# Linear attention and an MLP mixer: a new order of batch 1's first steps, new gates on the later quarters of w_ch2, token mixing of batch 1 in two parts

## The chip, the core and the metric

The kernel runs on one core of one Trainium2 chip. The core has five engines with an instruction queue each: PE (TensorE, matmuls; its weight loads are listed as PEld), DVE (VectorE), ACT (ScalarE), POOL (GpSimd) and SP (SyncE, here only an issuer of transfers). Transfers run on the core's 16 DMA engines, whoever issues them. The metric is the device time of one execution in microseconds, the median of several runs.

## The reference

For each of 8 batches, linear attention over 8 heads (576 rows, 64 columns a head), and then a mixer block: token mixing across the 576 rows, channel mixing across the 512 columns.

```python
def phi(x): return np.where(x > 0, x, np.exp(x) - 1.0) + 1.0
q_p, k_p = phi(q), phi(k)
kv  = einsum('bhsd,bhse->bhde', k_p, v)
z   = sum(k_p, axis=2)
num = einsum('bhsd,bhde->bhse', q_p, kv)
den = einsum('bhsd,bhd->bhs', q_p, z)[..., None] + 1e-06
x   = (num / den) as [batch, 576, 512]
h   = relu(x.T @ w_tok1) @ w_tok2        # w_tok1 576 x 256, w_tok2 256 x 576
u   = x + h.T
out = u + relu(u @ w_ch1) @ w_ch2        # w_ch1 512 x 1536, w_ch2 1536 x 512
```

All inputs and the output are float32 in memory; matmuls run in bfloat16 and sum in float32.

## The kernel before

**Tiles.** A batch's 576 rows are four tiles of 128 rows and a fifth, half full, of 64 (r = R = 4). The eight heads are two halves c = 0, 1 (loads, phi, transposes, kv), and a load of half of q, k or v is 576 KB. w_ch1 and w_ch2 are loaded in four quarters of 384 KB (as bfloat16); a quarter of w_ch2 holds three of the twelve row blocks kc, so quarter 1 is kc 0 to 2, quarter 2 is kc 3 to 5, quarter 3 is kc 6 to 8 and quarter 4 is kc 9 to 11.

**The steps of a batch.** phi (lines 146 to 170) takes exp on ACT (L149), an add and max on DVE (L155) and a min on DVE (L163). vcast (L174) casts v to bfloat16. qtr (lines 210 to 215) transposes phi(q) on PE (L200) and copies it from PSUM (L207). kv (lines 182 to 196) multiplies phi(k) by v, 72 small matmuls (L189), and copies the result on ACT (L195). nd (lines 223 to 246) does numerator and denominator of some row tiles of one half: matmuls (L230), then on DVE an add, a reciprocal and a product (L239, L241, L242) that writes x. mm1 (lines 297 to 306) is the first half of token mixing, ten matmuls (L303) over the five row tiles and a relu on ACT (L306); mm2_half (lines 343 to 361) is the second. mm3 (L531) and mm4 (L571) are channel mixing, whose results are evicted by ACT (L538) or DVE (L535) and, at the end, by mm4_end (L599).

**The order.** The program is written out by hand and each engine works through its own list in order. In the stage of the change, batch 0's channel mixing is the main work (the list `big`, lines 1007 to 1009: indices 0 to 11 are mm3 of the blocks mc, 12 to 23 are mm4 in the order of kc) and batch 1's first steps are put after numbered members of it (`at0` and `fill`, lines 1010 to 1028). The first two members of mm4, 12 and 13, do kc 0 and 1 for two row tiles each; 14 to 23 do one kc for all four row tiles, four matmuls each. They sum in four PSUM banks, the same four that mm3's blocks used. For batch 1 the order on PE before the change is: kc 0 and 1 (12 and 13), first transposes of q, kc 2, second transposes, kv, kc 3, nd00, kc 4, nd01, kc 5, nd10, kc 6, nd11, kc 7, nd20, kc 8, nd21, kc 9, mm1, kc 10, kc 11, mm2_half. The nd names give the pair of row tiles (0, 1, or 2 for the last tile) and the half.

**The transfers.** SP issues the loads of q, k and v in the order k, q, v for batch 1 (lines 956 to 958), then q, k, v for batch 2 (lines 960 to 962). POOL issues the weights' loads, since those are cast on the way. `after` (line 119) adds a wait for another transfer's landing. Before the change, batch 1's k waits for the first quarter of w_ch1, quarter 2 of w_ch2 waits for the first half of batch 1's q, quarters 3 and 4 follow it in POOL's list without a wait of their own, and the first half of batch 2's q waits for quarter 2.

## Time and profile before

| | |
|---|---|
| median of 3 runs | 250.88 us (250.22 to 251.24) |
| the profiled execution | 250.88 us, of which the traced span is 249.1 us |
| PE busy | 238.4 us (96% of the span), 2396 matmuls |
| DVE, ACT, POOL busy | 185.8, 140.7, 66.1 us |
| granted PE clock | 1.00 of full speed |
| read from memory, written | 35.85 MB, 9.44 MB |
| w_ch loads (8 of 384 KB), from issue to landing, median | 10.0 us |
| loads of k, q and v (halves), from issue to landing, medians | 6.0, 5.9 and 9.7 us |

The profile is of one execution. A line of the timeline gives the start in the span, the time from the first start to the last end of the merged instructions, the engine, the line of the kernel, the operation with what it writes and reads, and in brackets how long the engine had been idle and which work released it. Matmuls overlap: one of 128 x 512 is listed with 0.38 us, but four in a row start 0.86 us after each other. A line of the chain that ended last has the start, the duration, and the engine or transfer. A line of the windows has the stretch, its length, the busy time and the number of instructions of PE, PEld, DVE, ACT and POOL, the granted clock, the DMA share and the GB/s.

### The profile page before, as it was taken

The page shows a single profiled execution, that of the slowest core. Times are in us where ns is not written, and L with a number is a line of the kernel's source. Part 1 is how long each engine was busy: PE and PEld are TensorE (multiplying, and loading weights), DVE is VectorE, ACT ScalarE, POOL GpSimd, SP SyncE. Part 2 cuts the span into 40 slices and gives each one's busy share as a digit, 9 for nine tenths or more (in the row PEclk, how much of TensorE's full clock was granted, in tenths as well). Part 3 has the DMA queues.
Part 4 walks back from the last instruction along what each step waited for, and adds up shares of the span by engine and source line. Part 5 has one row for each costly group of instructions (what it writes and reads, how often), then busy time and mean ns, then how long its engine had stood idle before and what let it go on. Part 6 is the DMA issues. An engine that isn't in the chain of part 4 may idle for free.

```text
span 249.1 us, 5884 instructions
## 1 busy us (share of the span) xinstructions
PE 238.4 (96%) x2396; PEld 154.7 (62%) x2418; DVE 185.8 (75%) x328; ACT 140.7 (56%) x225; POOL 66.1 (27%) x76
## 2 busy tenths in 40 slices
PE   7799989999899999999999999999999999999994
PEld 3485445564768545765588545765577556888673
DVE  5984676889998378967594398858893859877853
ACT  4765681569775268745997168655953561275100
POOL 9750030296901700061004500051006100430000
PEclk9999999999999999999999999999999999999999
DMA  6999999999738994699938956699052702452036
GB/s 236 262 203 258 340 259 294 372 249 288 302 23 211 264 368 146 91 267 360 320 93 189 397 152 219 130 323 260 21 129 37 170 1 45 63 120 52 0 87 168
DMA packets 49771, 48.39 MB, mean 194 GB/s; under 512 B 30032, under 2 KB 35536, under 8 KB 49744
## 3 DMA queue, kind: packets, MB, share of 16 engines
q1 hardware_dynamic: 41648, 35.00, 48.6%
q0 software_dynamic: 7472, 12.22, 22.4%
q10 hardware_dynamic: 624, 0.79, 1.0%
q8 instruction: 19, 0.31, 0.5%
q14 instruction: 8, 0.07, 0.1%
HBM read 35.85 MB, written 9.44 MB: 182 GB/s over the span
## 4 chain that ended last, share of the span: by engine, by line
PE 76%; DMA 11%; DVE 5%; POOL 3%; issue 3%; SPq 0%; POOLq 0%; DVEq 0%
PE ps L780 22%; PE ps L531 21%; DMA wc<-in_moe_w_ch_dram 6%; PE ps L303 6%; DMA q_raw<-in_q_dram 5%; PE ps L571 5%; PE ps L316 4%; PE ps L734 4%; PE ps L704 4%; PE ps L558 2%; PE ps L580 2%; PE ps L545 2%; DVE y L155 2%; PE ps L259 1%; PE ps L189 1%
## 5 line engine op out<-in xcount | busy, mean ns | idle before, releaser
L531 PE MATMUL ps<-uT,wc 128*128 128x512 bf16 x332 | 76.0, 379 | 0.5 <-issue 0.2
L538 ACT ACTIVATE cr<-ps 128x512 bf16<-128x512 f32 x79 | 45.9, 600 | 32.9 <-PE ps L531 32.5
L531 PEld LDWEIGHTS <-wc 128*128 128x128 bf16 x336 | 32.0, 98 | 37.9 <-issue 1.1
L791 POOL TENSOR_TENSOR obuf<-obuf,q_raw 128x512 f32<-128x512 f32 x6 | 7.6, 1269 | 94.7 <-ACT w L785 74.5
L789 DVE TENSOR_TENSOR obuf<-ps,u 128x512 f32<-128x512 f32 x24 | 16.3, 687 | 11.8 <-PE ps L780 8.8
L780 PE MATMUL ps<-k_raw,v_raw 128*128 128x256 bf16 x216 | 24.9, 273 | 0.0
L780 PEld LDWEIGHTS <-cr 128*128 128x128 bf16 x216 | 21.1, 98 | 4.5
L780 PEld LDWEIGHTS <-v_raw 128*128 128x128 bf16 x216 | 21.0, 98 | 3.9 <-issue 0.4
L149 ACT ACTIVATE e<-q_raw 128x1152 bf16<-128x1152 f32 x16 | 18.2, 1159 | 8.1 <-DMA q_raw<-in_q_dram 8.1
L149 ACT ACTIVATE e<-k_raw 128x1152 bf16<-128x1152 f32 x16 | 18.2, 1163 | 3.9 <-DMA k_raw<-in_k_dram 3.8
L654 DVE TENSOR_TENSOR v_raw<-cr 128x768 bf16<-128x768 bf16 (+2 forms) x24 | 14.9, 619 | 5.0 <-ACT cr L538 5.0
L272 DVE TENSOR_TENSOR x<-ps,dens 128x768 bf16<-128x768 f32 x18 | 17.2, 958 | 0.6
L780 PE MATMUL ps<-wc,cr 128*128 128x256 bf16 x144 | 17.7, 273 | 0.0
L328 DVE TENSOR_TENSOR u<-ps,x 128x1024 bf16<-128x1024 f32 x12 | 14.7, 1222 | 1.8 <-PE ps L316 1.5
L155 DVE TENSOR_SCALAR y<-k_raw 128x1152 bf16<-128x1152 f32 x16 | 11.9, 769 | 4.8 <-DMA k_raw<-in_k_dram 4.8
L163 DVE TENSOR_TENSOR qp<-e,y 128x1152 bf16<-128x1152 bf16 x16 | 11.9, 756 | 3.6 <-ACT e L149 2.8
L163 DVE TENSOR_TENSOR kp<-e,y 128x1152 bf16<-128x1152 bf16 x16 | 11.8, 753 | 3.5 <-ACT e L149 3.4
L155 DVE TENSOR_SCALAR y<-q_raw 128x1152 bf16<-128x1152 f32 x16 | 13.4, 850 | 1.0 <-DMA q_raw<-in_q_dram 0.9
L303 PE MATMUL ps<-x,w 128*128 128x512 bf16 x49 | 13.8, 379 | 0.3
L174 ACT CAST vs<-v_raw 128x1152 bf16<-128x1152 f32 x12 | 13.5, 1160 | 0.0
L571 PE MATMUL ps<-wc,cr 128*128 128x512 bf16 x47 | 12.0, 379 | 1.0 <-DVE cr L535 0.7
L316 PE MATMUL ps<-ar,w2p 128*128 128x512 bf16 x44 | 11.6, 379 | 0.3
(161 smaller groups left out, 386.2 us busy)
## 6 DMA issues: line engine op xcount, KB each, us to landing
k_raw<-in_k_dram SPq DMA_DIRECT2D x16, 576.0 KB, 6.0
q_raw<-in_q_dram SPq DMA_DIRECT2D x16, 576.0 KB, 5.9
v_raw<-in_v_dram SPq DMA_DIRECT2D x14, 576.0 KB, 9.7
out_dram<-obuf POOLq DMA_DIRECT2D x12, 512.0 KB, 6.8
wc<-in_moe_w_ch_dram POOLq DMA_DIRECT2D x8, 384.0 KB, 10.0
out_dram<-obuf POOLq DMA_DIRECT2D x4, 256.0 KB, 5.2
cr<-in_v_dram POOLq DMA_DIRECT2D x2, 288.0 KB, 7.9
out_dram<-obuf POOLq DMA_DIRECT2D x4, 128.0 KB, 7.6
```

Of the source, the lines that this page charges most:

```text
L149: nc.scalar.activation(out=e, in_=f, func=AF.Exp)
L155: nc.vector.tensor_scalar(out=y, in0=f, scalar1=1.0, scalar2=1.0, op0=ALU.add, op1=ALU.max)
L163: live["phi"] = nc.vector.tensor_tensor(out=dst.transpose([0, 2, 1, 3]), in0=e.rearrange("p (i t d) -> p i t d", i=nj, t=T), in1=y.rearran ...
L272: nc.vector.tensor_tensor(out=xv[:, :, rc0:rc0 + 3], in0=v_[:, :, k0:k0 + 6, 0:D].rearrange("p i (q a) d -> p i q a d", a=2), in1=den[:, : ...
L303: nc.tensor.matmul(out=ps[:, mt], lhsT=w1t[:, b, ms] if r == R else w1[:, r, ms], rhs=x[b][:, r, :], start=(r == 0), stop=(r == R))
L316: nc.tensor.matmul(out=ps[:, i], lhsT=w2v(kt, r, b), rhs=ar[b][:, kt, :], start=(kt == 0), stop=(kt == NT - 1 and not add))
L531: nc.tensor.matmul(out=ps, lhsT=wc1[:, kj, 128 * mc:128 * mc + 128], rhs=uTj[b][:, kj] if n < 2 else uT[b][:, :, kj], start=(kj == 0), sto ...
L538: nc.scalar.activation(out=cr[b][:, mc, :], in_=ps, func=AF.Relu)
L571: nc.tensor.matmul(out=ps, lhsT=crt[:, kc, :] if t == 8 else cr[b][:, kc, 128 * r:128 * r + 128], rhs=wc2[:, kc, :], start=(kc == 0), stop ...
L654: nc.vector.tensor_tensor(out=s_[which - 1][:, ks], in0=x_, in1=y_, op=op)
L780: nc.tensor.matmul(out=live[tile_][:, j], lhsT=lhs[:, k_], rhs=rhs[:, k_], start=(first and j == 0 and k_ == 0), stop=(k_ == KH - 1), skip ...
L789: nc.vector.tensor_tensor(out=o, in0=live[tile_], in1=u[n % 2][:, d::2, HC[c]], op=ALU.add)
```

## The change

It has four parts.

1. Batch 1's steps take other places among the members of `big`. The order on PE becomes: kc 0 and 1, first transposes of q, kc 2, kc 3, second transposes, kc 4, kv, kc 5, nd00, kc 6, nd01, kc 7, nd10, nd11, kc 8, nd2, kc 9, mm1 without the last row tile, mm1's last row tile, kc 10, kc 11, mm2_half.
2. The last row tile's numerator and denominator are done for both halves at once (`nd_last`), and mm1 is issued in two parts: all row tiles but the last for both column blocks (8 matmuls), and then the last row tile (2 matmuls) and the relus.
3. The copies of the second transposes are split between DVE and ACT (they were both on DVE), and the cast of v's second half is split, one pair of heads on DVE and one on ACT (it was all on ACT).
4. Quarter 2 of w_ch2 waits for the second half of batch 1's k, quarter 3 for the first half of its v (POOL's list keeps their order, and quarter 4 follows), and the first half of batch 2's q waits for the second half of batch 1's v.

```diff
--- before.py
+++ after.py
@@ -169,8 +169,8 @@
         phi_add(nm, n, 2 * c, 2)
         phi_end(nm, n, 2 * c, 2)
 
-    def vcast(n, c, copy=nc.scalar.copy):
-        js = slice(2 * c, 2 * c + 2)
+    def vcast(n, c, copy=nc.scalar.copy, js=None):
+        js = slice(2 * c, 2 * c + 2) if js is None else slice(js[0], js[-1] + 1)
         copy(out=vs[:, js, :, 0:D],
              in_=raw["v", rb(n)][:, js].rearrange("p j (t d) -> p j t d", t=T))
 
@@ -207,12 +207,12 @@
         put(out=v_[:, :, c, ts[0]:ts[-1] + 1].transpose([0, 2, 1, 3]),
             in_=tp[:, 0:len(ts)].rearrange("p t (a s) -> p t a s", a=2))
 
-    def qtr(n, c, put=nc.scalar.copy):
+    def qtr(n, c, put=2 * [nc.scalar.copy]):
         tp = two16()
         for h, ts in enumerate(TS):
             qtr_mm(c, ts, tp[:, h])
         for h, ts in enumerate(TS):
-            qtr_put(n, c, ts, tp[:, h], put)
+            qtr_put(n, c, ts, tp[:, h], put[h])
 
     def qtr_dma(n):
         for a in range(2):
@@ -244,6 +244,24 @@
                 "p r (h d) -> p r h d", h=HG),
             in0=v_[:, :, :, 0:D],
             in1=den[:, :, :, None].to_broadcast([128, m, HG, D]), op=ALU.mult)
+
+
+    def nd_last(n):
+        b = n % 2
+        ps = banks()
+        for c in range(2):
+            o = ps[:, c, 0:4 * D1].rearrange("p (i a e) -> p a i e", i=2, a=2)
+            for a in range(2):
+                t0 = D * (T * (2 * a + c) + 2 * R - b)
+                nc.tensor.matmul(out=o[:, a], lhsT=qT[b][:, t0:t0 + 128], rhs=kvbd[b][:, c, a],
+                                 start=True, stop=True)
+        v_ = ps[:, :, 0:HG * D1].rearrange("p c (h e) -> p c h e", h=HG)
+        den = work.tile([128, 2, HG], FP32, name="den", tag="den")
+        nc.vector.tensor_scalar(out=den, in0=v_[:, :, :, D], scalar1=EPS, scalar2=None, op0=ALU.add)
+        nc.vector.reciprocal(out=den, in_=den)
+        nc.vector.tensor_tensor(
+            out=x[b][:, R].rearrange("p (c h d) -> p c h d", c=2, h=HG), in0=v_[:, :, :, 0:D],
+            in1=den[:, :, :, None].to_broadcast([128, 2, HG, D]), op=ALU.mult)
 
 
 
@@ -294,15 +312,17 @@
         at = D * (T * kt + 2 * r - (b if r == R else 0))
         return w2p[:, at:at + 128]
 
-    def mm1(n):
+    def mm1(n, rs=range(R1)):
         b = n % 2
-        ps = banks(4 if n > 1 else None)
+        if rs[0] == 0:
+            live["mm1"] = banks(4 if n > 1 else None)
+        ps = live["mm1"]
         for mt in range(NT):
             ms = slice(128 * mt, 128 * mt + 128)
-            for r in range(R1):
+            for r in rs:
                 nc.tensor.matmul(out=ps[:, mt], lhsT=w1t[:, b, ms] if r == R else w1[:, r, ms],
                                  rhs=x[b][:, r, :], start=(r == 0), stop=(r == R))
-        for mt in range(NT):
+        for mt in range(NT) if rs[-1] == R else ():
             nc.scalar.activation(out=ar[b][:, mt, :], in_=ps[:, mt], func=AF.Relu)
 
     def mm2(n, rs, add=False):
@@ -956,24 +976,26 @@
     for nm in "kqv":
         for c in range(2):
             landed[nm + "1", c] = load(nm, 1, c, c_in[0] if nm == "k" and c == 0 else None)
-    c2_in += [after(load_wc2(i), landed["q1", 0] if i == 1 else None) for i in range(1, NB)]
+    c2_in += [after(load_wc2(i), landed[{1: ("k1", 1), 2: ("v1", 0)}[i]] if i < 3 else None) for i in range(1, NB)]
     for nm in "qkv":
         for c in range(2):
-            load(nm, 2, c, c2_in[1] if nm == "q" and c == 0 else None)
+            load(nm, 2, c, landed["v1", 1] if nm == "q" and c == 0 else None)
 
 
     def steps(n):
 
         out_ = [("kv", lambda: kv(n, range(2)))] if n < 2 else []
         if n == 1:
-            puts = [nc.scalar.copy, nc.vector.tensor_copy if n == 1 else nc.scalar.copy]
+            puts = [2 * [nc.scalar.copy], [nc.vector.tensor_copy, nc.scalar.copy]]
             out_ += [(f"qt{c}", lambda c=c: qtr(n, c, puts[c])) for c in range(2)]
-        for i, rs in enumerate(([0, 1], [2, 3], [4])) if n < 2 else ():
+        for i, rs in enumerate(([0, 1], [2, 3])) if n < 2 else ():
             for g in range(2):
                 out_.append((f"nd{i}{g}", lambda g=g, rs=rs: nd(n, g, rs)))
+        if n < 2:
+            out_ += [("nd2", lambda: nd_last(n)), ("mm1a", lambda: mm1(n, range(R)))]
         if n > 1:
             out_.append(("nd", lambda: nd_all(n)))
-        out_.append(("mm1", lambda: mm1(n)))
+        out_.append(("mm1", lambda: mm1(n, range(R1) if n > 1 else [R])))
         if n > 1:
             out_ += [("mm2a", lambda: mm2(n, [0, 1])), ("mm2b", lambda: mm2(n, [2, 3]))]
             if n % 2:
@@ -1007,20 +1029,22 @@
     big = [lambda mc=mc: mm3(0, mc, range(2, 4), dve=mc == 3) for mc in range(4)] + \
         [lambda mc=mc: mm3(0, mc, dve=mc in (6, 9)) for mc in range(4, NCH)] + \
         [lambda kc=kc: m4_0(kc) for kc in range(NCH)]
-    at0 = {"qt0": 13, "qt1": 14, "vc": 13, "kv": 14, "nd00": 15, "nd01": 16, "nd10": 17,
-           "nd11": 18, "nd20": 19, "nd21": 20, "mm1": 21}
+    at0 = {"qt0": 13, "vc0": 15, "qt1": 15, "vc1": 15, "kv": 16, "nd00": 17, "nd01": 18,
+           "nd10": 19, "nd11": 19, "nd2": 20, "mm1a": 21, "mm1": 21}
     fill = []
     for ex, ad, en, nm, c in ((2, 2, 3, "k", 0), (5, 5, 6, "k", 1), (8, 8, 9, "q", 0),
                               (11, 11, 12, "q", 1)):
         fill += [(ex, lambda nm=nm, c=c: phi_exp(nm, 1, 2 * c, 2)),
                  (ad, lambda nm=nm, c=c: phi_add(nm, 1, 2 * c, 2)),
                  (en, lambda nm=nm, c=c: phi_end(nm, 1, 2 * c, 2))]
-    late = [("vc", lambda: vcast(1, 0, nc.vector.tensor_copy)), ("vc", lambda: vcast(1, 1))]
+    late = [("vc0", lambda: vcast(1, 0, nc.vector.tensor_copy)),
+            ("vc1", lambda: vcast(1, 1, nc.vector.tensor_copy, [2])),
+            ("vc1", lambda: vcast(1, 1, nc.scalar.copy, [3]))]
     fill += [(21, lambda g=g: phi("q", 2, g)) for g in range(2)]
     fill += [(22, lambda: qtr_dma(2)), (22, lambda: load_all(3, "q"))]
     fill += [(22, lambda: weight_sums((tf, B12, B11), (tb[1], B22, tf)))]
     first = steps(1)
-    for nm, fn in first[1:2] + late + first[2:3] + first[0:1] + first[3:]:
+    for nm, fn in first[1:2] + late[:1] + first[2:3] + late[1:] + first[0:1] + first[3:]:
         fill += [(at0[nm], fn)]
     fill += [(23, fn) for fn in (
         lambda: mm4_end(0, 0), lambda: mm4_end(0, 1), lambda: mm2_half(1, 0),
```

## The prediction

> **What bounds the kernel now.** I read the page's busy row first, then the chain that ended last in order of time, then the PE timeline around the changed steps, then who waited there. The first row says where to look:
>
> ```profile
> PE 238.4 (96%) x2396; PEld 154.7 (62%) x2418; DVE 185.8 (75%) x328; ACT 140.7 (56%) x225; POOL 66.1 (27%) x76
> ```
>
> TensorE is the bound, and its granted clock is 1.00 in every stretch from 20 to 42 us, so only its idle time or its work can change the end. From 54 us on the chain is nearly all PE, so a shift X of batch 1's end shifts the end of the kernel by X. The chain shows two transfers ahead of the place that is changed:
>
> ```profile
> 18.97 12.43 DMA q_raw<-in_q_dram
> ...
> 31.93 5.87 DMA wc<-in_moe_w_ch_dram
> 37.80 0.04 issue
> 37.84 0.38 PE ps L571
> ```
>
> The reader sees q of batch 1 (first half) land at 31.40, the second quarter of w_ch2 issued at 31.93 because of that landing, and PE's block kc=3 released by it at 37.84. The PE timeline gives every gap:
>
> ```profile
> 31.79 0.39 PE L571 MATMUL ps<-wc,cr 128*128 128x512 bf16 x1
> 32.83 1.67 PE L571 MATMUL ps<-wc,cr 128*128 128x512 bf16 x7 [0.65 <-DVE cr L535]
> 34.34 0.67 PE L200 MATMUL ps<-identity,qp 128*128 128x128 bf16 x9
> 34.84 1.03 PE L571 MATMUL ps<-wc,cr 128*128 128x512 bf16 x4
> 35.71 0.67 PE L200 MATMUL ps<-identity,qp 128*128 128x128 bf16 x9
> 36.30 0.48 PE L189 MATMUL ps<-vs,kp 64*64 64x65 bf16 x36
> 37.11 0.48 PE L189 MATMUL ps<-vs,kp 64*64 64x65 bf16 x36 [0.32 <-ACT vs L174]
> 37.84 1.02 PE L571 MATMUL ps<-wc,cr 128*128 128x512 bf16 x3 [0.25 <-DMA wc<-in_moe_w_ch_dram]
> 38.70 0.40 PE L230 MATMUL ps<-kvbd,qT 128*128 128x130 bf16 x4
> ```
>
> Matmuls overlap, so I take a cost from start to start. In the chain four L571 take 0.86 us, so a block of mm4 is 0.86. Nine transposes are 0.50 (34.34 to 34.84), 72 kv matmuls 0.71, four nd matmuls 0.24, ten mm1 matmuls 2.15. The stretch from the first L571 (31.79) to the first matmul of mm2_half (48.95) is 17.16 us. Its work is 12 x 0.86 + 2 x 0.50 + 0.71 + 5 x 0.24 + 2.15 = 15.38. So PE idles 1.78 us there: 0.82 at 31.79 to 32.83 (less one matmul of 0.22), 0.45 before 37.11 (36.30 + 0.36), 0.37 before 37.84, and crumbs. **That is all the change can win.**
>
> **Part 1: the order on PE.** Nothing is removed but one of six nd rounds in name: nd2 issues the same four matmuls as nd20 and nd21, so PE's work stays 15.38. On DVE it replaces 2 x (0.16 + 0.18 + 0.42) by 0.17 + 0.20 + 0.69, 0.46 less, beside PE blocks: the nd chain on DVE ends at 45.23 and mm1 reads the last row tile only at 45.92. The split of the second q transpose's copies (DVE 0.41, ACT 0.69 or 0.59 in the L207 rows) and of v's cast (half of DVE's 0.758, half of ACT's 1.16) is worth nothing while kv is late for another reason; without that it cuts 0.5 us from the wait before 37.11. The 0.82 stays: the DVE eviction L535 stands behind phi's add, which waited for q's landing at 31.40, and both come before anything moved. The moves are: block kc=3 ahead of the second transposes, kc=4 ahead of kv. So kc=3 is wanted at 32.83 + 1.51 + 0.50 + 0.86 = 35.70 instead of 37.47, and kc=6, behind nd00 and no longer behind nd10, one block and one nd earlier relative to kv. Kv now has two blocks (1.72 us) of cover for its v.
>
> **Part 2: the queues.** Here the sum is decided. The trace's landing records (16 completions of each transfer, one by each DMA engine) show one engine about 1 us behind the others: k of batch 1, second half, 27.08 to 27.51 on fifteen, 28.43 on the last; v, second half, to 34.92 and 35.87. Landing means that last engine. It ends q at 31.40 and 33.02, v at 34.44 and 35.87, and the second to fourth quarters at 37.80, 39.69, 41.82: a half of q or v costs it 1.42 us alone, a quarter 1.9, and it never rests. So an earlier request there does not add bandwidth; it only changes the order.
>
> New gates: quarter 2 after k's second half (28.43) instead of q's first half (31.40), hence issued at 28.43 + 0.53 (the 31.40 to 31.93 of before) = 28.96. When does that engine take it up? Issued at 31.93 it landed at 37.80, so its 1.9 us began at 35.9, 3.9 after the issue, with v's transfers running. The lower end: at once behind the first quarter, which ends at 31.74. I take 28.96 + 3.9 = 32.9, the row that is the same transfer under the same load. From there it shares with v. Sharing has rows too: between 28.43 and 31.40 a half took 2.97 instead of 1.42, beside the first quarter, which took 4.2 for itself (27.54, the end of the small transfer ahead of it, to 31.74). So quarter 2 lands at 32.9 + 4.2 = 37.1, v's first half at 33.02 + 2.97 = 36.0 instead of 34.44, and v's second at 33.02 + 1.42 + 1.43 + 1.9 = 37.8, some 38.0 with the loss of sharing. Quarter 3 is new in its gate: after v's first half, 36.0 + 0.53 = 36.5, where it had been issued at 32.69. Its landing: at best when that engine is free, 38.0 + 1.9 = 39.9; at worst 5.87 after the issue, 42.4 (or 42.9 where v is at 36.5). Between them stands the row of the other fifteen engines: they landed quarter 2 at 36.47 to 36.89, 4.8 after its issue although idle by 34.9. I take 36.5 + 4.8 = 41.3. While the queue starts up, the DMA share falls:
>
> ```profile
> 30.00:32.00 2.00, 1.91 (x8) 0.70 (x8) 1.07 (x2) 1.18 (x3) 0.07 (x1) 1.00 1.05 402
> 32.00:34.00 2.00, 1.35 (x7) 0.57 (x6) 2.00 (x4) 2.00 (x4) 2.00 (x3) 1.00 0.94 325
> 34.00:36.00 2.00, 2.00 (x22) 1.29 (x21) 1.41 (x3) 1.85 (x4) 0.36 (x1) 1.00 0.92 170
> ```
>
> The last number is GB/s: 402 falls to 170 as POOL's three quarters (issued 31.93 to 34.35) begin. The new gates let POOL start this twice. Behind quarter 3's wait on POOL stand only quarter 4 (wanted by kc=9, four blocks later) and work from 48.4 on. q of batch 2 now waits for v's second half (38.0) instead of quarter 2 (37.80): no change for SP's queue, whose later loads follow it, and none for exp on ACT, which had it at 43.95.
>
> The Trainium skill, "DMA: Bandwidth & Descriptors", section "Anatomy of one DMA — SWDGE (gpsimd) path", gives about 2.0 us plus bytes by 436 GB/s for such a transfer, by which 384 KB take an estimated 2.9 us against the 5.87 of the chain; by it quarters 2 and 3 would land near 32 and 38, nothing but the 0.82 would be left of the stalls, and the time would be near 250.0. The row is under load and I go by the row. The same page, section "Queues, rings and completion order", has each DMA engine go round robin between queues by packet, which speaks against this change, since quarter 2 then holds up v; the 2.97 against 1.42 agrees.
>
> **The sum.** Block kc=2 ends at 35.70 and kc=3 waits to 37.1 (1.4, new). Then kc=3 37.96, transposes 38.46, kc=4 39.32, kv without a wait (v's casts done by 38.0 + 0.65 = 38.7) 40.03, kc=5 40.89, nd00 41.15 (its kvbd copies, 0.76 on ACT, are hidden by kc=5). kc=6 waits for quarter 3 until 41.3 (0.15). From there to mm2_half: six blocks 5.16, four nd 0.96, mm1 2.15 = 8.27, with DVE's nd rounds (1.07 each) done at 45.8, under mm1a. So mm2_half begins at 49.6 instead of 48.95: +0.65, some +0.7 with crumbs. The profiled execution is 250.88 (span 249.1 and 1.78 around it), which is also the median shown. **Forecast 251.6 us**, +0.3%. The waits of 0.45 and 0.37 are removed and one of 1.4 put in their place.
>
> **Rivals.**
> - A, the gain: quarter 2 begins at 31.74 and lands at 31.74 + 4.2 = 35.9, so kc=3 waits 0.2. v's halves land at 36.5 and 38.0, kv waits some 0.2 for the last cast (38.7), kc=6 is reached at 40.2, and quarter 3 is there (39.9). mm2_half at 40.2 + 8.27 = 48.5: -0.45, 250.4; with no stall but the 0.82, -0.95, 249.9. For it: the ring is free for it by order of issue. Against: the 3.9 us from issue to work of the same transfer.
> - B, slower: quarter 3 decides. It is wanted at 40.2 to 41.2, earlier than the 41.30 of before, and asked for at 36.5 to 37.0 instead of 32.69. If it needs the 5.87 of quarter 2, it lands at 42.4 to 42.9 and mm2_half is at 50.7 to 51.2: +1.7 to +2.2, 252.6 to 253.1, centre 252.8. It costs anything from a landing at 40.7 (48.95 - 8.27) and over 0.5% from 41.95. For it: the dip in the windows, and q of batch 2 arriving at 40 beside it. Against: v is over by 38, so that nothing need hold it.
> - C, the change does not do what it says: quarter 2 still lands at 37.8 behind v. Then the order alone acts: kc=3 from 37.84, kc=6 at 41.85, mm2_half at 50.1: +1.2, 252.1. Against: it is issued 3 us earlier.
>
> **How the numbers follow.** Forecast 0.42, A 0.20, B 0.30, C 0.08. Half a per cent (1.25 us) is about what a measurement of this kernel can tell from no change. Slower by more: B nearly whole (0.28), half of C and the tail of the forecast (0.05), 0.33. Faster by more asks for a gain of 1.25 out of 1.78 with the 0.82 kept, so it is left 0.05. Within: 0.62. The range takes in A's centre and B's upper half: 250.2 to 253.0.
>
> **What would show it.** In the new PE timeline: the gaps before 37.11 and 37.84 gone; a gap of about 1.4 before kc=3 released by the DMA of wc (step right; 0.2 is A, 2.1 is C); the gap at 32.83 still 0.82 (larger: quarter 2 came early enough to hold up q, which I priced at nothing); a gap before kc=6, after nd00, released by wc (0 to 0.5 forecast, over 1 is B). The first POOL issue at 28.96, the second where v's first half lands, 36.0. I am wrong if quarter 2 is taken up within 2 us of its issue, or if the stages after 54 us do not simply shift.

## The result and the profile after

The changed kernel takes **254.22 us** (median of 4 runs, 253.15 to 254.41), beside 251.06 us (250.22 to 251.30) of the kernel before: ratio 1.0123, 95% interval 1.0086 to 1.0161. It is 3.2 us slower; 251.6 was forecast, and the measured time lies above the range of 250.2 to 253.0. Here and below medians and ranges are of all executions, but ratios and intervals only of those within 1.5% of the fastest of the same kernel, which leaves out the profiled executions of e2, e6 and e12, so that of these only the stretch up to 66 us is read. The profiled execution of the changed kernel is 253.15 us (span 251.4), 2.27 us above that of before. In it the lines have moved by up to 20: mm3 is L551, mm4 L591, mm2_half L372, POOL's sums L661.

The row of the busy times shows the same work, 1.0 us more of it listed on PE in a span 2.3 us longer:

```profile
PE 239.4 (95%) x2396; PEld 155.0 (62%) x2418; DVE 185.9 (74%) x325; ACT 140.8 (56%) x226; POOL 66.4 (26%) x76
```

The chain that ended last passes through quarter 2 of w_ch2, as before, and now also through a transposing transfer of u in batch 2:

```profile
18.43 10.33 DMA k_raw<-in_k_dram
29.30 7.86 DMA wc<-in_moe_w_ch_dram
37.20 1.02 PE ps L591 x4
...
83.32 3.62 DMA uT<-u
86.98 1.90 PE ps L551 x8
```

Quarter 2 is asked for at 29.30 instead of 31.93 and lands at 37.16 instead of 37.80. A request 2.63 us earlier brought 0.64 us. The PE timeline of the changed kernel in the stage of the change:

```profile
31.92 1.95 PE L591 MATMUL ps<-wc,cr 128*128 128x512 bf16 x8
33.70 0.67 PE L200 MATMUL ps<-identity,qp 128*128 128x128 bf16 x9
34.20 1.03 PE L591 MATMUL ps<-wc,cr 128*128 128x512 bf16 x4
37.20 1.02 PE L591 MATMUL ps<-wc,cr 128*128 128x512 bf16 x4 [1.97 <-DMA wc<-in_moe_w_ch_dram]
38.06 0.67 PE L200 MATMUL ps<-identity,qp 128*128 128x128 bf16 x9
38.56 1.03 PE L591 MATMUL ps<-wc,cr 128*128 128x512 bf16 x4
39.52 0.99 PE L189 MATMUL ps<-vs,kp 64*64 64x65 bf16 x72
...
44.16 0.40 PE L230 MATMUL ps<-kvbd,qT 128*128 128x130 bf16 x4 [0.19 <-DVE x L242]
...
50.23 0.27 PE L372 MATMUL ps<-x,identity 128*128 128x256 bf16 x1
```

The gap of 0.82 at kc 0 and 1 is gone, and so are the two ahead of kv's second half and of kc=3. In their place stands one gap ahead of kc=3: block kc=2 ends at 35.06 (34.20 + 0.86) and kc=3 starts at 37.20, **2.1 us** later (the bracket counts 1.97, from the modelled end of the last matmul). kv is listed in one piece with 0.99, and there is no gap ahead of kc=6 at 41.60. mm2_half begins at 50.23 instead of 48.95, **+1.28**. At 68.27, where the last 32 small matmuls on the row tails (the fifth tiles) of batches 0 and 1 start behind batch 2's numerators and denominators, it is +1.97, and from 87 us to the end a constant +2.24.

The windows show the same dip in what is moved while POOL's transfers start, 142 GB/s where it was 170, with the DMA share at 1.06 or more:

```profile
32.00:34.00 2.00, 2.00 (x15) 0.99 (x14) 1.50 (x3) 2.00 (x4) 0.10 (x1) 1.00 1.12 319
34.00:36.00 2.00, 1.23 (x11) 0.60 (x9) 1.43 (x2) 1.24 (x3) 1.77 (x2) 1.00 1.07 142
36.00:38.00 2.00, 0.80 (x4) 0.38 (x4) 0.00 (x0) 0.00 (x0) 0.00 (x0) 1.00 1.06 174
```

In the last of the three, PE has four matmuls in 2 us, and DVE, ACT and POOL do nothing while it waits for the transfer.

### The profile page after: what moved, and what is told of

It is laid out like the page before. It is cut to its first block, busy times and chain, and to the rows that moved or that the text cites. A ratio compares the mean times of both kernels' runs of the same rounds, so it can differ in the third digit from the quotient of the medians.

```text
span 251.4 us, 5884 instructions
## 1 busy us (share of the span) xinstructions
PE 239.4 (95%) x2396; PEld 155.0 (62%) x2418; DVE 185.9 (74%) x325; ACT 140.8 (56%) x226; POOL 66.4 (26%) x76
## 4 chain that ended last, share of the span: by engine, by line
PE 75%; DMA 12%; DVE 5%; POOL 3%; issue 2%; ACT 1%; SPq 0%; POOLq 0%; DVEq 0%
PE ps L551 22%; PE ps L800 21%; DMA wc<-in_moe_w_ch_dram 7%; PE ps L323 6%; DMA k_raw<-in_k_dram 4%; PE ps L336 4%; PE ps L754 4%; PE ps L724 4%; PE ps L591 3%; PE ps L578 2%; PE ps L600 2%; PE ps L565 2%; PE ps L189 2%; PE ps L277 2%; DMA uT<-u 1%
## 5 line engine op out<-in xcount | busy, mean ns | idle before, releaser
L551 PE MATMUL ps<-uT,wc 128*128 128x512 bf16 x332 | 76.0, 379 | 1.2 <-DVE cr L555 0.6
L551 PEld LDWEIGHTS <-wc 128*128 128x128 bf16 x336 | 32.0, 98 | 38.9 <-issue 1.9
L155 DVE TENSOR_SCALAR y<-k_raw 128x1152 bf16<-128x1152 f32 x16 | 12.5, 806 | 5.4 <-DMA k_raw<-in_k_dram 5.4
L591 PE MATMUL ps<-wc,cr 128*128 128x512 bf16 x46 | 11.6, 379 | 2.2 <-DMA wc<-in_moe_w_ch_dram 2.0
L174 ACT CAST vs<-v_raw 128x1152 bf16<-128x1152 f32 (+1 forms) x12 | 13.0, 1120 | 0.0
```

The source lines that it names most:

```text
L155: nc.vector.tensor_scalar(out=y, in0=f, scalar1=1.0, scalar2=1.0, op0=ALU.add, op1=ALU.max)
L551: nc.tensor.matmul(out=ps, lhsT=wc1[:, kj, 128 * mc:128 * mc + 128], rhs=uTj[b][:, kj] if n < 2 else uT[b][:, :, kj], start=(kj == 0), sto ...
L591: nc.tensor.matmul(out=ps, lhsT=crt[:, kc, :] if t == 8 else cr[b][:, kc, 128 * r:128 * r + 128], rhs=wc2[:, kc, :], start=(kc == 0), stop ...
```

## The theories

**T1, the order.** kc=3 now stands ahead of the second transposes and of kv, so PE comes to it 2.4 us sooner in the program (35.06), and quarter 2 lands near 37 whatever its gate. The wait is the loss, and what hangs on batch 1's steps makes it grow.

**T2, the gates (rival).** The new gates slow the transfers of q and v, or let quarter 2 and v hold each other up; with the old gates the new order would cost nothing.

**T3, the later stage (rival).** The loss at the end arises mainly after 55 us, between DVE and POOL or at the transposing transfer of u, and the stage of the change only sets it off.

A table for what follows, each row from one profiled execution, in us from the start of its span: landing of the first half of batch 1's q, landing of quarter 2, PE's longest gap between kc=2 and kc=5, start of mm2_half, and start of the last 32 small matmuls on the row tails (L545 or L565). The last column is the ratio of the times to those of the kernel before on the same chip.

| kernel | q | quarter 2 | gap | mm2_half | row tails | ratio [95%] |
|---|---|---|---|---|---|---|
| before | 31.40 | 37.80 | 0.32 | 48.95 | 66.30 | |
| changed | 30.29 | 37.16 | 1.97 | 50.23 | 68.27 | 1.0123 [1.0086, 1.0161] |
| e0 | 30.11 | 36.77 | 1.95 | 49.85 | 67.87 | 1.0136 [1.0087, 1.0185] |
| e1 | 31.07 | 37.29 | 1.79 | 50.37 | 68.40 | 1.0132 [1.0080, 1.0184] |
| e2 | 30.93 | 37.34 | 1.88 | 49.78 | 67.13 | 1.0040 [1.0003, 1.0078] |
| e3 | 30.04 | 36.43 | 1.50 | 49.51 | 66.97 | 1.0088 [1.0055, 1.0122] |
| e4 | 30.34 | 36.56 | 0.32 | 47.70 | 65.57 | 1.0024 [0.9993, 1.0055] |
| e5 | 31.03 | 37.25 | 0.60 | 48.90 | 66.22 | 1.0009 [0.9974, 1.0044] |
| e6 | 30.32 | 36.73 | none | 47.67 | 65.70 | 1.0029 [0.9999, 1.0059] |
| e8 | 31.57 | 35.67 | none | 50.67 | 68.01 | 1.0145 [1.0097, 1.0192] |
| e9 | 30.06 | 36.78 | 0.32 | 47.93 | 65.28 | 0.9987 [0.9971, 1.0004] |
| e11 | 30.63 | 36.84 | 0.60 | 48.62 | 65.93 | 0.9997 [0.9968, 1.0026] |
| e12 | 30.08 | 36.62 | none | 47.71 | 65.73 | 1.0048 [1.0010, 1.0087] |
| e13 | 30.53 | 37.09 | none | 48.21 | 65.68 | 1.0012 [0.9980, 1.0045] |
| e14 | 30.51 | 37.44 | none | 48.61 | 66.08 | 0.9994 [0.9967, 1.0022] |
| e15 | 30.39 | 36.96 | none | 47.83 | 65.86 | 0.9989 [0.9966, 1.0012] |

e10 left no profile that can be read; its ratio is 1.0095 [1.0069, 1.0121].

## The experiments

**e0: the changed kernel again.**

> The changed kernel once more, for a second profile and more times, since its profiled execution (253.15 us) lay 1 us below its other three (254.1 to 254.4). Theory (PE waits for the second quarter of w_ch2): 253 to 254.5 us; the new profile again has a gap of 1.5 to 3 us on PE ahead of block kc=3, released by the transfer of wc, and the quarter lands at 37 to 38 us. Rival (the queues themselves, two separate starts of POOL's transfers): the gap stands ahead of kc=6 or in the loads of batch 2 in this one.

Measured: 254.12 us (252.55 to 255.11). The gap ahead of kc=3 is 1.95, quarter 2 landed at 36.77. The loss and its place are those of the first profile.

**e1: the new order alone.** Order, `nd_last` and splits as changed, gates as before.

```diff
-    c2_in += [after(load_wc2(i), landed[{1: ("k1", 1), 2: ("v1", 0)}[i]] if i < 3 else None) for i in range(1, NB)]
+    c2_in += [after(load_wc2(i), landed["q1", 0] if i == 1 else None) for i in range(1, NB)]
-            load(nm, 2, c, landed["v1", 1] if nm == "q" and c == 0 else None)
+            load(nm, 2, c, c2_in[1] if nm == "q" and c == 0 else None)
```

> The new order, nd_last, mm1 in two parts and the split copies, with the old gates of the transfers. Theory: quarter 2 lands at 37.8 as before the change, kc=3 is wanted at some 35.5 and waits 2.3 us, everything behind it on PE is later by 0.6 us than in the changed kernel: 253.5 to 255 us. Rival (the gates cost the time): the gates are the old ones, so the time is that of the kernel before, 250.5 to 251.5.

Measured: 254.23 us, the whole loss. Its PE timeline has the same gap at the same place, although quarter 2 was asked for 2.3 us later (31.61):

```profile
34.52 1.03 PE L591 MATMUL ps<-wc,cr 128*128 128x512 bf16 x4
37.34 1.02 PE L591 MATMUL ps<-wc,cr 128*128 128x512 bf16 x4 [1.79 <-DMA wc<-in_moe_w_ch_dram]
```

The gates neither cause the loss nor soften it. T2 falls.

**e2: the new gates alone.** The kernel before with the two gate lines of the change (e1's diff, the other way round).

> The old order with the new gates. Theory: kv's second half waits for v until about 37.5 (0.5 us more than before), kc=3 follows at 37.9 and finds its quarter landed at 37.2: 250.5 to 251.5 us. Rival (the gates cost the time): 252.5 us and more, with a wait for quarter 3 ahead of kc=6.

Measured: 252.80 us, ratio 1.0040. v's second half lands at 36.97 instead of 35.87, held up by quarter 2, and ACT's undivided cast of it holds up kv; kc=3 comes behind it and finds its quarter there:

```profile
35.83 0.48 PE L189 MATMUL ps<-vs,kp 64*64 64x65 bf16 x36
38.20 0.48 PE L189 MATMUL ps<-vs,kp 64*64 64x65 bf16 x36 [1.88 <-ACT vs L174]
38.61 1.04 PE L571 MATMUL ps<-wc,cr 128*128 128x512 bf16 x4
```

The gates alone move the wait from one transfer to the other. The time is above the forecast of 250.5 to 251.5, but the rival's wait ahead of kc=6 is not there, and by the ratios the gates cost less than the order.

**e5: the old places.** Gates as before (e1's lines), every step back at its old place among the blocks; `nd_last`, mm1 in two parts and the splits stay.

```diff
-    at0 = {"qt0": 13, "vc0": 15, "qt1": 15, "vc1": 15, "kv": 16, "nd00": 17, "nd01": 18,
-           "nd10": 19, "nd11": 19, "nd2": 20, "mm1a": 21, "mm1": 21}
+    at0 = {"qt0": 13, "vc0": 13, "qt1": 14, "vc1": 14, "kv": 14, "nd00": 15, "nd01": 16,
+           "nd10": 17, "nd11": 18, "nd2": 19, "mm1a": 21, "mm1": 21}
```

> The old gates and the old places of the transposes, v's casts, kv and the nd rounds; new are only nd_last, mm1 in two parts and the split copies and casts. Theory (the places of kc=3 and kc=4 ahead of the second transposes and kv are what costs): the time of the kernel before, 250.5 to 251.5, kv's second half 0.3 us sooner, kc=3 at 37.8 as before. Rival (the last row tile in one round and mm1 in two parts, or the split, cost): 252.5 us and more, with gaps on PE around mm1.

Measured: 250.53 us beside 249.91 (ratio 1.0009, [0.9974, 1.0044]): the kernel before. With e1 this puts the loss in the places, and prices `nd_last`, mm1's two parts and the splits at nothing that can be measured.

**e6: the new order without the wait.** In the changed kernel, blocks kc 3 to 5 of batch 0 read the first quarter's rows instead of quarter 2's, which are there; the product of three row blocks of w_ch2 is left out, one taken twice.

```diff
-                rhs=wc2[:, kc, :], start=(kc == 0), stop=(kc == NCH - 1))
+                rhs=wc2[:, kc - 3 if wait and 3 <= kc < 6 else kc, :],
+                start=(kc == 0), stop=(kc == NCH - 1))
```

> The changed kernel, but blocks kc=3 to 5 of batch 0 multiply the first quarter of w_ch2 instead of the second, so nothing on PE waits for quarter 2 there (the part left out: the product of three row blocks of w_ch2 with batch 0). All transfers and all instructions are those of the changed kernel. Theory (PE's wait for quarter 2 is the loss): no gap ahead of kc=3; kv then waits for v's second half (36 us and its casts), some 0.3 us; mm2_half 1.5 to 2 us sooner than in the changed kernel and the end 2 to 2.5 us sooner, 251 to 252 us. Rival (the transfers' new order costs in itself, elsewhere): 253.5 us and more.

Measured: 250.84 us, ratio 1.0029 [0.9999, 1.0059]. kc=2 and kc=3 are one row of 8 matmuls, and mm2_half starts at 47.67, 2.56 earlier than in the changed kernel:

```profile
33.77 1.89 PE L591 MATMUL ps<-wc,cr 128*128 128x512 bf16 x8
35.49 0.67 PE L200 MATMUL ps<-identity,qp 128*128 128x128 bf16 x9
...
47.67 0.27 PE L372 MATMUL ps<-x,identity 128*128 128x256 bf16 x1
```

So the wait for quarter 2 is most of the loss, and T1 holds for it. Everything else in the change, the late v included, comes to 0.3%, with an interval from nothing to 0.6%. What follows mm2_half does not go away with the wait: from mm2_half to the row tails it is 18.03 here and 18.04 in the changed kernel, against 17.35 in the kernel before.

**e8: quarter 2 without a gate.** The changed kernel, quarter 2 asked for at 16.67 behind the first quarter.

```diff
-    c2_in += [after(load_wc2(i), landed[{1: ("k1", 1), 2: ("v1", 0)}[i]] if i < 3 else None) for i in range(1, NB)]
+    c2_in += [after(load_wc2(i), landed["v1", 0] if i == 2 else None) for i in range(1, NB)]
```

> The changed kernel without any gate on quarter 2 of w_ch2: POOL issues it right behind quarter 1, ahead of batch 1's loads. Theory (the slowest DMA engine is busy without a pause until 38 us, so an earlier quarter 2 makes q and v later by the 1.9 us that it takes): quarter 2 lands at 33 to 34 us and there is no gap ahead of kc=3, but q's first half lands at 32 to 33 and PE waits before kc=0 (0.82 before, 0 to 0.5 in the changed kernel) for 1 to 2 us, and kv waits for v at 37.5 to 38: 252.5 to 254.5 us, no better than the changed kernel by more than 1 us. Rival (the late quarter 2 is a mere question of its gate): 250 to 251.5 us, no gaps.

Measured: 254.28 us, no better than the changed kernel. Quarter 2 lands at 35.67, 1.5 earlier (33 to 34 was expected), and the price is paid by all others: q 31.57 and 33.72, v 35.83 and 37.13, quarter 3 40.77 (39.05 in the changed kernel), quarter 4 45.88 (41.69). Its PE timeline has three smaller gaps for the one that went:

```profile
33.01 1.67 PE L591 MATMUL ps<-wc,cr 128*128 128x512 bf16 x7 [0.79 <-DVE cr L555]
...
40.81 1.02 PE L591 MATMUL ps<-wc,cr 128*128 128x512 bf16 x4 [0.36 <-DMA wc<-in_moe_w_ch_dram]
...
45.92 0.38 PE L591 MATMUL ps<-wc,cr 128*128 128x512 bf16 x1 [1.07 <-DMA wc<-in_moe_w_ch_dram]
```

So the request that was moved forward moved the others back, and the time is the same.

**e3: POOL's first sums earlier.** POOL's "sums" are differences of blocks of w_ch2. In the changed kernel, the first six, which wait for phi(q) of batch 2, wait for its first half instead of its second.

```diff
-    fill += [(21, lambda g=g: phi("q", 2, g)) for g in range(2)]
+    def phi_q2(g):
+        phi("q", 2, g)
+        if g == 1:
+            live["phi"] = live["phi_q2"]
+        live["phi_q2"] = live["phi"]
+
+    fill += [(21, lambda g=g: phi_q2(g)) for g in range(2)]
```

> The changed kernel, but POOL's first six differences of w_ch2 blocks wait for the first half of phi(q) of batch 2 instead of the second, so POOL begins them some 1.5 us earlier. Theory (the DVE op on k of batch 2 at 56.13 us took 1.59 instead of 0.98 us because POOL's last difference was still running): that op is 0.8 to 1.0 us long again and the end comes 0.6 us sooner than in the changed kernel, unless POOL then lengthens the DVE ops on q of batch 2 by as much. Rival (it is later for PE's sake, POOL is beside it): no change, within 0.2 us in the profile.

Measured: 253.59 us, ratio 1.0088, beside 1.0136 of e0 (the intervals overlap, so at the end the gain is not shown). The first add of phi(k) of batch 2 takes 0.89 us instead of 1.59, and the 0.69 that the changed kernel loses between mm2_half and the row tails (50.23 to 68.27 against 48.95 to 66.30 is 18.04 against 17.35) is gone: 49.51 to 66.97 is 17.46. But the collision came back at another place. The last minimum of phi(q) of batch 2 now runs beside POOL's first sums and takes twice its 0.76:

```profile
48.79 1.52 DVE L163 TENSOR_TENSOR qp<-e,y 128x1152 bf16<-128x1152 bf16 x1
...
55.53 1.56 DVE L155 TENSOR_SCALAR y<-k_raw 128x1152 bf16<-128x1152 f32 x2
```

**e4: POOL's sums later.** The kernel before, with a POOL memset of 0.52 us ahead of its first sums.

```diff
+        if abc[0][0] is tf and not live.get("pad"):
+            live["pad"] = after(nc.gpsimd.memset(w2[:, 0, 0:512], 0.0), first[0])
```

> The kernel before, with one POOL instruction of about 0.5 us (a memset of a part of w_tok2's tile that is no longer read) put ahead of POOL's first differences of w_ch2 blocks and behind the same wait. Theory (a DVE op from SBUF to SBUF goes on until POOL's running difference ends): the first add of phi(k) of batch 2 lasts 1.4 to 1.6 us instead of 0.98, and PE's block of the row tail behind nd of batch 2 starts 0.5 us later than in the kernel before: 251.4 us where before has 250.9. Rival (POOL is beside the path): no change, within 0.2 us in the profile.

Measured: 250.63 us, ratio 1.0024 [0.9993, 1.0055]. The collision is made in the kernel before: the pair of adds takes 2.17 instead of 1.66 (the first alone 1.50 instead of 0.98), and mm2_half to the row tails is 17.87 (47.70 to 65.57) instead of 17.35. That is 0.5 in this stage; at the end it is not told from nothing.

**e11 and e12: quarter 2 in three transfers** of one row block each, so that kc=3 waits for its own rows alone. e12 is the changed kernel with it; e11 is e5 with it (gate as before).

```diff
+    def load_wc2_rows(i, m=1):
+        return nc.gpsimd.dma_start(
+            out=wc2[:, i:i + m, :],
+            in_=moe_w_ch2[128 * i:128 * (i + m), :].rearrange("(k p) d -> p k d", p=128))
...
+    c2_in += [[after(load_wc2_rows(3 + j), landed["k1", 1] if j == 0 else None) for j in range(3)][2]]
+    c2_in += [after(load_wc2(i), landed["v1", 0] if i == 2 else None) for i in range(2, NB)]
```

> The old gates and old places with the split casts, nd_last and mm1 in two parts, and quarter 2 of w_ch2 as three transfers of one row block each (kc=3, 4, 5). Theory (kc=3 waits for a whole quarter of which it needs a third): kc=3's third lands at 36.5, 1.3 us ahead of the old quarter; kv's second half starts at some 36.7 to 37.0 and kc=3 right behind it, mm2_half 0.5 to 0.8 us sooner than before: 249.4 to 250.4 us by a kernel before of 250.0 to 250.9, so 0.2 to 0.3% faster. Rival (three transfers cost more than one on the slowest DMA engine): no change, or slower by up to 0.5 us.

> The changed kernel with quarter 2 as three transfers, the first with its gate. Theory: kc=3's third lands at 34.5 to 35.7 instead of 37.2, the gap of 2.1 us ahead of kc=3 shrinks to 0.6 or less, kc=4 and kc=5 find theirs landed or wait for some tenths, and the kernel is 1.3 us or more faster than the changed one: 251 to 252.5 us. Rival (the order itself, with nd rounds close together, costs): 253 us and more although the gap is gone.

Measured, e11: 250.53 us, ratio 0.9997. The thirds land at 35.60, 36.24 and 36.84, but kv stands ahead of kc=3 there and waits 0.60 for DVE's cast of v; the gain of 0.2 to 0.3% that I expected is not there. Measured, e12: 252.34 us, ratio 1.0048 [1.0010, 1.0087], by the ratios 0.75% better than the changed kernel, as expected. The thirds land at 34.61, 36.13 and 36.62, the gap ahead of kc=3 is gone (kc=2 and kc=3 are one row of 8 matmuls), and mm2_half starts at 47.71:

```profile
33.81 1.89 PE L591 MATMUL ps<-wc,cr 128*128 128x512 bf16 x8
35.54 0.67 PE L200 MATMUL ps<-identity,qp 128*128 128x128 bf16 x9
36.17 1.02 PE L591 MATMUL ps<-wc,cr 128*128 128x512 bf16 x4
```

**e9 and e10: without the transposing transfer of u in batch 2.** In the kernel before (e9) and the changed one (e10), the first four blocks of mm3 of batch 2 read batch 1's transposes; their right product is left out.

```diff
-                             rhs=uTj[b][:, kj] if n < 2 else uT[b][:, :, kj],
+                             rhs=uTj[b][:, kj] if n < 2 else
+                             uT[1 if n == 2 and mc < 4 else b][:, :, kj],
```

> The kernel before, but the first four blocks of channel mixing of batch 2 read the transposes of batch 1 instead of those of batch 2 (that product is left out), so PE doesn't wait for the second transposing transfer of batch 2's u, which in some profiles had one of its 16 engines land 1.5 us behind the others, when a 16 KB packet of the instruction queue ran beside it. Theory (that wait is 0 or about 2 us from one execution to the next, in both kernels): the times draw together, 249.5 to 250.7, median some 250. Rival (the scatter is from elsewhere): the times are as scattered as those of the kernel before.

> The changed kernel with the same product left out. Theory (1.3 us at the wait for quarter 2, 0.6 us where DVE meets POOL's sums; the rest of the measured 3.1 us is the wait for the transposing transfer, which hit more of its executions): 252 to 252.8 us, drawn together, 2.0 to 2.5 us above the kernel before with that product left out. Rival (a further loss of its own): 3 us and more above it.

Measured: 249.68 us (249.33 to 250.70) and 252.52 us (251.63 to 254.23; one execution of 502.81 us, its profiled one, is not used), on the same chip. The ratio of the two medians is 1.0114, 2.8 us, between what I expected (2.0 to 2.5) and the rival (3 and more): without any wait for that transfer the change costs nearly as much as with it. In the kernel before, the transfer spreads the times: the executions that the ratio uses ranged from 249.55 to 252.35 on that chip, e9's from 249.33 to 250.70. That e10's would draw together did not come true. Three rows show the wait, in the kernel before, the changed kernel and e1, in this order:

```profile
84.75 1.90 PE L531 MATMUL ps<-uT,wc 128*128 128x512 bf16 x8
```
```profile
86.98 1.90 PE L551 MATMUL ps<-uT,wc 128*128 128x512 bf16 x8 [0.31 <-DMA uT<-u]
```
```profile
88.87 1.90 PE L551 MATMUL ps<-uT,wc 128*128 128x512 bf16 x8 [2.06 <-DMA uT<-u]
```

**e13, e14, e15: both mended.** e13 is e12 with e3's edit, the whole computation; e14 is e13 and e15 is e12 with e10's edit (the same product left out).

> The changed kernel with quarter 2 of w_ch2 asked for in three transfers of one row block each, and POOL's first six differences of w_tok rows released by the first half of phi(q) of batch 2 instead of its last. If the loss is the wait ahead of kc=3 and the meeting of POOL's sums with DVE's add of phi(k): no gap ahead of kc=3, the first add of phi(k) of batch 2 near 0.9 us, batch 1's end and the block of mm4 at about 65 us some 1.2 us sooner than in the kernel before, and the time 249.0 to 249.6 beside 250.2 to 251.1 of the kernel before. If the gain of 1.2 us at 55 us is given back after 65 us (rival: the second transposing transfer of u sets the start of channel mixing of batch 2, whatever comes before it), the time is that of the kernel before, 250.2 to 251.1, with a gap of 1.5 us or more there.

> As e13_thirds_pool_early, and the first four blocks of channel mixing of batch 2 read batch 1's transposes of u, so that they wait for no transposing transfer of batch 2; their right product is left out. It stands beside the kernel before with the same product left out (249.68, one job earlier). If the order is worth what the stage from 30 to 65 us shows: 1.2 us less than that, 248.2 to 248.9. If something else behind 65 us takes the gain back: 249.4 or more.

> As e12_thirds_after (quarter 2 in three transfers, POOL's sums where the change has them), with the same product left out as in e14. If the meeting of POOL's sums with DVE's add costs what the stage at 65 us showed, 0.4 to 0.6 us more than e14_e13_no_ut, 248.7 to 249.4. If the meeting costs nothing at the end: the same as e14 within 0.2 us.

Measured: e13 250.93 us (ratio 1.0012 [0.9980, 1.0045]), e14 250.35 us (0.9994 [0.9967, 1.0022]), e15 250.29 us (0.9989 [0.9966, 1.0012]), beside 250.36 of the kernel before. The gain of 1.2 us that I expected is not there: **mended, the new order is as fast as the kernel before, and not faster.** e13's time is the one that the rival gave, but the rival's reason is not shown: the wait for the transposing transfer is 0.46 in e13's profile, not 1.5, and e14, which has none, is no faster than e9, the kernel before with the same product left out (0.9987). e14 and e15 are alike in time, where I expected 0.4 to 0.6 us between them. In e13 and e14 the meeting of POOL and DVE stands at phi(q) (1.53 instead of 0.76), and the two adds take 1.57 in e13 instead of 2.27. Of these 0.70, 0.55 is left at the row tails (17.47 from mm2_half in e13 and e14, 18.02 and 18.03 in e12 and e15), but in the profiles of e13 and e14 mm2_half itself starts 0.4 to 0.9 later; whether e3's edit has a part in that is not shown:

```profile
47.49 1.53 DVE L163 TENSOR_TENSOR qp<-e,y 128x1152 bf16<-128x1152 bf16 x1
...
54.24 1.57 DVE L155 TENSOR_SCALAR y<-k_raw 128x1152 bf16<-128x1152 f32 x2
```

No version beats the kernel before; e13 is, by the ratios, 1.1% faster than the changed one. T3 holds for a part: the meeting adds 0.5 to 0.7 us behind mm2_half. It comes with the new order and not with the wait, since e6, e12 and e15 have it without the wait.

## Why the prediction was wrong, point by point

**The step that failed** is "From 54 us on the chain is nearly all PE, so a shift X of batch 1's end shifts the end of the kernel by X". That is a misreading of the chain. From 51.3 to 66.3 us it lies on DVE, with gaps that it lists as issue, and only from there on it is nearly all PE. From the kernel before:

```profile
53.57 1.29 DVE obuf L599 x2
54.85 1.58 DVE y L155 x2
...
65.97 0.29 DVE x L279
66.30 1.95 PE ps L545 x32
```

So the start of mm2_half on PE, which the sum followed, is not what sets the end. In all sixteen profiles the row tails start 10.54 to 10.55 us after the end of DVE's first add of phi(k) of batch 2, the first of the two in the second line above. From the row tails on a shift does reach the end: in the thirteen profiles that are read to their end, the time is the start of the row tails, plus the wait for the transposing transfer, plus 184.4 to 184.8. That the stages after 54 us might not simply shift, the prediction itself named as a sign of being wrong. Two terms of the sum were off as well, the path to mm2_half and the base. Of the 2.27 us between the two profiled executions, 0.65 was forecast, and the rest comes from these rows:

- **kc=3: the time right, in part by luck.** 37.1 forecast, 37.20 measured; quarter 2's landing 37.1 and 37.16. Its first packets stand at 32.62, 3.3 us after the request (3.9 taken), and the slowest engine ended it 4.5 later (4.2 taken). But the 3.9 is no property of the transfer: in the kernel before, the first packets stand at 33.40, 1.5 after the request. The wait is 2.1 instead of 1.4 because PE came sooner (35.06, not 35.70): q landed at 30.29, and the 0.82 that I kept in the sum was not there.
- **The path to mm2_half: 0.5 short.** From kc=3 I counted 12.5 us, it took 13.03. kv took 0.2 more (0.92 from its start to the next block's in e0, where no matmul is missing from the trace, against 0.71), probably since its last pair waits for ACT's half cast at 39.30, which stands behind ACT's copy of the transposes; the blocks on both sides of it took up to 0.1 more each; nd11 came 0.36 late behind DVE's x of nd01, since nd10 and nd11 now follow each other without a block between. I had priced all of these at nothing. The 0.15 ahead of kc=6 was not needed. So +1.28 at mm2_half, not +0.65.
- **After mm2_half: the shift grows.** I followed PE and not DVE. DVE's five nd rounds start at 41.87, where the six of before started at 39.14, and end 1.98 later, at 47.21. (The sum had them done at 45.8; its own terms give 46.7: nd00 at 40.89, 0.44 to DVE's first step as in the rows of before, and five times 1.07.) phi(q) of batch 2 follows, and POOL's six sums wait for it. So POOL moves by 1.97 while DVE's later work, tied to PE, moves by 1.36, and what hardly touched before now meets. POOL's and DVE's rows in the kernel before:

```profile
48.39 3.38 POOL L641 TENSOR_TENSOR q_raw<-wc 128x512 f32<-128x512 bf16 x3 [14.03 <-DVE qp L163]
51.73 3.40 POOL L641 TENSOR_TENSOR k_raw<-wc,q_raw 128x512 bf16<-128x512 bf16 x3
```
```profile
54.77 1.66 DVE L155 TENSOR_SCALAR y<-k_raw 128x1152 bf16<-128x1152 f32 x2
```

and in the changed kernel:

```profile
50.36 3.38 POOL L661 TENSOR_TENSOR q_raw<-wc 128x512 f32<-128x512 bf16 x3 [14.59 <-DVE qp L163]
53.70 3.40 POOL L661 TENSOR_TENSOR k_raw<-wc,q_raw 128x512 bf16<-128x512 bf16 x3
```
```profile
56.13 2.27 DVE L155 TENSOR_SCALAR y<-k_raw 128x1152 bf16<-128x1152 f32 x2
```

POOL ends at 55.13 and 57.10, and in both the first add ends 0.62 after that (0.98 and 1.59 long). So it does in thirteen of the sixteen profiles; in the other three (e5, e8, e11) POOL was done earlier, and the add took 0.87 to 0.90. DVE's work behind it moves by the same 1.97, and so do the matmuls that it releases (the first row is before's, the second the changed kernel's):

```profile
66.30 1.95 PE L545 MATMUL ps<-uTt,wc 128*128 128x128 bf16 x32 [0.56 <-DVE x L279]
```
```profile
68.27 1.89 PE L565 MATMUL ps<-uTt,wc 128*128 128x128 bf16 x31 [0.79 <-DVE x L297]
```

That takes the shift from +1.28 to +1.97; in their profiles e3 takes most of the growth away and e4 makes 0.5 of it. The wait for the transposing transfer adds 0.27.
- **The base.** The profiled execution of before was a late one in this stretch: e4 and e9 have the same code up to there and start mm2_half at 47.70 and 47.93, not 48.95, with q at 30.34 and 30.06 instead of 31.40 and no gap at kc 0 and 1. "All the change can win" was 1.78 of idle time, of which 1.0 was not there in these two. e9, with the old order and gates, and e0, with the new ones, show the change best. Quarter 2 was asked for at 30.60 and at 28.92 and landed at 36.78 and 36.77, and in both kc=3 starts right behind it (e9's rows, then e0's):

```profile
36.82 1.02 PE L572 MATMUL ps<-wc,cr 128*128 128x512 bf16 x4 [0.17 <-DMA wc<-in_moe_w_ch_dram]
...
47.93 0.27 PE L352 MATMUL ps<-x,identity 128*128 128x256 bf16 x1
```
```profile
36.81 1.02 PE L591 MATMUL ps<-wc,cr 128*128 128x512 bf16 x4 [1.95 <-DMA wc<-in_moe_w_ch_dram]
...
49.85 0.27 PE L372 MATMUL ps<-x,identity 128*128 128x256 bf16 x1
```

The 0.7 us that the sum gave to the earlier request is not there, and what had been done ahead of the landing (the second transposes, kv) now stands behind it: 11.11 us from kc=3 to mm2_half in the kernel before and e9, 13.03 and 13.04 in the changed kernel and e0. So mm2_half moves by 1.92, the end of the nd rounds by 2.61 and the row tails by 2.59, which fits the 2.8 us between e9 and e10; these are single executions, on two chips.

**The rivals.** C named the mechanism: "the order alone acts", kc=3 waits 2.1. Its condition (quarter 2 at 37.8) did not come, but against e9 quarter 2 landed no sooner either; its wait came, and its 252.1 was short by what follows mm2_half and by the base. I had given it a chance of 0.08. B was wrong in its place: quarter 3 landed at 39.05, 1.7 sooner than any cost, since v's first half landed at 33.60 (36.0 forecast) and quarter 3 was asked for at 33.90. A was wrong: its landing of quarter 2 at 35.9 is reached only without any gate (35.67 in e8), and there at everyone else's cost.

**The page on transfers.** I weighed the Trainium skill, "DMA: Bandwidth & Descriptors", section "Anatomy of one DMA — SWDGE (gpsimd) path", by which 384 KB would take an estimated 2.9 us; it took 7.86 from request to landing, and the row was the better guide. **The meeting of POOL and DVE** fits another page of the Trainium skill, "SBUF — State Buffer", section "SBUF: two separate sides", which says that a DVE operation in some modes, or with two inputs from SBUF, and one of GpSimd share a pair of ports as a lock, which the one that starts first holds for its whole instruction. The rows agree in kind: in the changed kernel the add starts 0.18 us after the start of POOL's last sum (55.95, 1.16 long) and ends 0.6 us after that sum's end, and in e13 the minimum of phi(q) ends 0.6 us after a sum of POOL's that takes 1.60 instead of 1.15. That the ports are the reason is not shown by these runs. By that page the meeting could have been looked for; I had not followed POOL's gate, so I did not look.

**What stays open.** The first packets of quarter 2 (or of its first third) stand at 32.4 to 33.4 in every profile but e8's, for requests from 28.6 to 31.9; what they wait for is not shown. Nor is why the transposing transfer of u is late in some executions: in the three profiles with a wait near 2 us that are read to their end (e1, e4, e8), a packet of 16 KB of the instruction queue takes 1 us on one DMA engine at 83.8 to 86.6, beside that transfer, and in most of those with little or no wait it stands behind 89.6 (the changed kernel, e0, e3, e5, e9, e11). But in the kernel before it stands at 84.23, beside the transfer too, and there is no wait. That is a coincidence in time; nothing was tried that moves it.

## What to carry to other kernels

A block that waits for a transfer belongs behind the work that is ready, and the time of its landing, not of its request, says where: kc=3 was moved 2.4 us forward to a transfer that landed at 36.8 whether it was asked for at 28.9 or at 30.6. Here, splitting the transfer to what the block reads (e12) was worth more than asking for it earlier, which only delayed the others (e8). The chain is read line by line between the change and the end, also where one engine has most of it: here DVE had 15 us, and the change came through there. And a shift on the bounding engine is followed through every engine that is tied to it by a gate (here DVE, then POOL, then DVE again), since two engines that shift by different amounts can meet; an idle gap that is to be won should be seen in more than one execution.

## What the runs showed of the hardware

- DVE's cast of half of v (128 x 576) took 0.744 us, that of the whole (128 x 1152) 0.757: halving the columns won nothing, where I had expected 0.38. ACT's fell from 1.16 to 0.68.
- The last of a transfer's sixteen landings, one by each DMA engine, is the one that counts: quarter 2's were at 34.86 to 36.63 on fifteen DMA engines and at 37.16 on the last.
- A DVE add of 0.76 us took 1.59 beside POOL's sums, and a DVE minimum of 0.76 took 1.53.
- The same code started mm2_half at 47.70, 47.93 and 48.95 in three executions (e4, e9 and the kernel before), with the granted clock at 1.00 from 30 to 50 us: the landings of q moved by 1.3 us, and the steps behind them with it.
